# Window masks of four attention units added to the scores in quarter tiles of the TensorE, with new instruction orders

## The chip, the cores and the metric

One core of a Trainium2 chip runs the whole kernel. A core has a matrix engine (TensorE, PE in the profile), a vector engine (VectorE, DVE), an activation engine (ScalarE, ACT), a general engine (GpSimd, POOL) and a queue engine that starts most transfers (SyncE, SP). Each works through its own line of instructions in order; semaphores tie the lines together. PEld in the profile is the loading of matmul weights, which overlaps PE. PSUM is the memory that matmuls write (8 banks per partition), SBUF the one that everything else uses. The metric is the device time of one execution in microseconds, the median of the runs.

## What is computed

Windowed attention with four "sink" keys feeds a channel-mix layer (RWKV's), for 4 batches, 8 heads, 768 tokens, head size 64, model width 512 and hidden width 1024:

```python
scores = q @ k.T / sqrt(64)
keep = is_sink | ((rel >= 0) & (rel < 128))       # rel = query position - key position
a = softmax(where(keep, scores, -1e9))
x = concat_heads(a @ v)                           # (4, 768, 512)
x_prev = x shifted by one token (zero first)
xk = mu_k * x + (1 - mu_k) * x_prev
xr = mu_r * x + (1 - mu_r) * x_prev
k = max(xk @ w_k, 0)
out = sigmoid(xr @ w_r) * ((k * k) @ w_v)
```

## The kernel before

**Tiling.** The work is cut into 12 units: unit u is batch u // 3 and the 256 tokens of third T = u % 3. A unit has four head pairs c. For each unit the kernel loads q, k and v (`ks`, `qs`, `vs`), casts them to bf16 (`kb`, `qb`, `vb`), transposes q and k (`kt`, `qt`; on PE with a copy out of PSUM, or by a transposing transfer for the keys of units 5 to 11 and the queries of 7 to 11), makes the scores, takes the exponential on ACT (L917, `e`), masks it on DVE, multiplies by the values on PE (L950; a column of ones gives the row sums), and divides on DVE (`rec` L964, `x` L967). The mix step transposes `x` to `xt` (PE and a copy, or a transfer for units 6 and 8 to 11) and forms `td` (the difference of neighbouring tokens), `xk` and `xr` on DVE. The channel mix ("ffn") of a unit is 8 hidden products (operations `kp`, four matmuls of 256 columns each, L1117), a relu (`rl`) and a square (`kk`), two gates (`rp`, four matmuls of 512 columns, L1148, `th`), and value products (`vp`, four matmuls of 512 columns each, L1166; two operations per 128 tokens), then `ob` and a store.

**Scores.** Scores of a head pair lie transposed, keys on partitions, queries along the free dimension, in one `sc` tile of [128, 2, 512] floats: two banks, one per head a. There are two such tiles, so one PE operation makes the scores of two head pairs. The 512 columns of a head are four blocks of 128: old keys for the first 128 queries (block 0), the unit's first 128 keys for its first and second 128 queries (blocks 128 and 256), its second 128 keys for its second 128 queries (block 384). For T = 0 block 0 does not exist. The matmuls (L845) run in tiles of 64 x 64: head a takes the row half, 64 keys take the column half, which gives four tiles; quarter blocks that the window never reaches are not computed (the memset L567 gives one of them a zero). Unit 0 (`WHOLE`) alone uses 64 x 128.

**Masks.** For T > 0 operation `masked` (L931) multiplies the exponentials of one head pair, [128, 4, 256] bf16, by a 0/1 mask: 32 operations of 1,024 elements per partition; for T = 0 it uses `mask0`: 16 operations of 768. The kernel also holds a way to add a bias by a full 128 x 128 matmul (`biased`), for units in `BIAS`, which is empty.

**Order.** Every step is an operation with a number (the order of the calls of `P.op`). `ORDER` writes out by hand, for each engine, the order of its operations by number. `CHOICE` names the engine of operations that can run on more than one (casts, copies, relus, stores, and whether a sink product runs in 64 x 64 tiles, "PE/tiles", or in the full array, "PE/full"). `schedule` walks those lines with modelled costs; from its modelled clocks come the physical buffer of each tile and the filler matmuls that keep PE occupied while it would wait (L1226, L1229, L1232; only before 28.5 us by `fill_until`). `FETCH` and the line with `0.58 * cost` belong to that model; they issue nothing themselves. Semaphores follow from the order and the buffers.

**Operations that the prediction names** (number before / after the change): 89 is the cast on DVE of the last quarter of w_v (L654); 236 is the second half of a value product of unit 0 (L1166), which reads it. 286 / 279 is the `xk` of unit 2, head pair 1 (L1040); 374 / 367 is the first hidden product of unit 2 (L1117), which reads it. 215 / 212 is the first hidden product in PE's line (unit 0), 81 / 82 the cast of the second quarter of w_k that it reads.

Of the kernel before, what the change touches and what calls it, by code (L numbers as in the profile page):

```python
# [9 lines left out]
BF16 = mybir.dt.bfloat16  # L10
# [8 lines left out]
    80: "ACT", 81: "POOL", 82: "ACT", 83: "POOL", 84: "POOL", 85: "ACT", 86: "ACT",  # L19
    88: "ACT", 90: "DVE", 96: "POOL", 98: "DVE", 99: "DVE", 101: "DVE", 102: "ACT",  # L20
    103: "ACT", 129: "POOL", 132: "DVE", 135: "POOL", 141: "ACT", 144: "DVE", 151:
    "DVE", 160: "PE/full", 172: "PE/full", 183: "POOL", 186: "DVE", 189: "POOL",
    192: "POOL", 195: "ACT", 196: "DVE", 198: "DVE", 242: "PE/full", 265: "DVE",
    268: "DVE", 271: "POOL", 273: "DVE", 274: "POOL", 277: "DVE", 278: "ACT", 352:
    "POOL", 355: "POOL", 361: "DVE", 380: "DVE", 428: "POOL", 432: "POOL", 438:
    "ACT", 496: "PE/full", 511: "POOL", 516: "ACT", 517: "ACT", 587: "POOL", 591:
    "ACT", 592: "ACT", 628: "POOL", 661: "POOL", 663: "POOL", 665: "ACT", 666:
    "ACT", 675: "DVE", 736: "POOL", 741: "ACT", 785: "POOL", 810: "POOL", 815:
    "DVE", 855: "POOL", 888: "DVE", 889: "ACT", 929: "POOL", 945: "PE/full", 998:
    "DVE", 1002: "DVE", 1006: "DVE", 1010: "DVE", 1019: "POOL",  # L30
# [7 lines left out]
BIAS = ()  # L38
# [7 lines left out]
LOW = -30000.0  # L46

FETCH = (17500.0, 28500.0, 36900.0, 47800.0, 57300.0, 66500.0, 78000.0, 85500.0,
         96000.0, 104000.0, 113000.0, 126000.0, 135000.0, 147000.0, 161000.0)
# [5 lines left out]
TOGETHER = 2  # L55
# [3 lines left out]
WHOLE = (0,)  # L59
# [35 lines left out]
    ),  # L95
    "DVE": (
# [1193 lines left out]
```

## Time and profile before

| | us |
|---|---|
| median of 3 runs | 166.36 |
| lowest and highest run | 165.06, 167.31 |
| span of the profiled execution (first to last instruction) | 163.8 |
| PE busy in it | 154.4 |
| DVE busy | 148.4 |
| ACT busy | 121.4 |
| POOL busy | 32.7 |

The page gives the profiled execution by its span; what lies around it is the 2.6 us between the span and the median of the runs. In a timeline row the columns are start, length, engine, line, operation, output<-inputs, shapes and count, then the idle time before it and what ended that; neighbouring instructions of one kind are merged. An instruction's record includes the draining of its pipeline, so rows of one engine overlap, and the distance from a start to the next start is what it takes of the engine's line.

### The profile page before, as it was taken

The page shows a single profiled execution, that of the slowest core. Times are in us where ns is not written, and L with a number is a line of the kernel's source. Part 1 is how long each engine was busy: PE and PEld are TensorE (multiplying, and loading weights), DVE is VectorE, ACT ScalarE, POOL GpSimd, SP SyncE. Part 2 cuts the span into 40 slices and gives each one's busy share as a digit, 9 for nine tenths or more (in the row PEclk, how much of TensorE's full clock was granted, in tenths as well). Part 3 has the DMA queues.
Part 4 walks back from the last instruction along what each step waited for, and adds up shares of the span by engine and source line. Part 5 has one row for each costly group of instructions (what it writes and reads, how often), then busy time and mean ns, then how long its engine had stood idle before and what let it go on. Part 6 is the DMA issues. An engine that isn't in the chain of part 4 may idle for free.

```text
span 163.8 us, 4680 instructions
## 1 busy us (share of the span) xinstructions
PE 154.4 (94%) x1845; PEld 100.8 (62%) x1845; DVE 148.4 (91%) x383; ACT 121.4 (74%) x198; POOL 32.7 (20%) x61
## 2 busy tenths in 40 slices
PE   7989779899999999999999999999999999999991
PEld 2446458675468558777656666855385756578450
DVE  2589999999999999999999999998898989999931
ACT  3779899999999998999996689882499694152020
POOL 6643543222731022111103001032000100101001
PEclk9999999999999999999999999999999999999998
DMA  4999999999999999999997998979999963251032
GB/s 138 250 334 275 400 346 205 362 397 338 200 289 238 265 233 225 196 179 189 276 233 174 254 196 218 242 188 119 239 162 201 268 79 98 57 203 64 0 144 112
DMA packets 78821, 35.16 MB, mean 215 GB/s; under 512 B 68744, under 2 KB 71056, under 8 KB 78800
## 3 DMA queue, kind: packets, MB, share of 16 engines
q1 hardware_dynamic: 78384, 33.56, 85.8%
q0 software_dynamic: 400, 1.31, 2.3%
q8 instruction: 14, 0.23, 0.6%
q14 instruction: 7, 0.06, 0.1%
q10 hardware_dynamic: 16, 0.00, 0.0%
HBM read 24.12 MB, written 6.29 MB: 186 GB/s over the span
## 4 chain that ended last, share of the span: by engine, by line
PE 69%; DVE 11%; DMA 10%; SPq 5%; issue 2%; ACT 1%; POOL 0%; DVEq 0%; POOLq 0%
PE bank L1117 22%; PE bank L1166 19%; PE bank L1148 9%; PE bank L950 6%; DMA ks<-in_k_dram 5%; PE sc L845 4%; DMA kt<-kb 4%; DVE e L931 3%; SPq L462 3%; PE bank L1232 3%; DVE xk L1040 2%; DVE x L967 2%; PE bank L903 1%; SPq L479 1%; PE bank L991 1%
## 5 line engine op out<-in xcount | busy, mean ns | idle before, releaser
L1117 PE MATMUL bank<-xk,wk_sb 128*128 128x256 bf16 x384 | 47.3, 273 | 0.7 <-ACT rl L1127 0.5
L917 ACT ACTIVATE e<-sc 128x1024 bf16<-128x1024 f32 (+1 forms) x48 | 44.4, 966 | 3.4 <-PE sc L845 3.3
L1166 PE MATMUL bank<-wv_h,kk 128*128 128x512 bf16 x184 | 44.9, 379 | 0.0
L1117 PEld LDWEIGHTS <-wk_sb 128*128 128x128 bf16 x384 | 36.2, 98 | 7.0 <-issue 0.9
L931 DVE TENSOR_TENSOR e<-e,mask 128x1024 bf16<-128x1024 bf16 (+1 forms) x48 | 31.7, 676 | 0.0
L1127 ACT ACTIVATE rl<-bank 128x512 bf16<-128x512 f32 x43 | 25.1, 606 | 8.1 <-PE bank L1117 7.9
L1154 ACT ACTIVATE th<-bank 128x512 f32<-128x512 f32 x24 | 14.3, 608 | 18.2 <-PE bank L1148 11.4
L1166 PEld LDWEIGHTS <-kk 128*128 128x128 bf16 x184 | 17.0, 98 | 16.4
L1148 PE MATMUL bank<-wr_sb,xr 128*128 128x512 bf16 x96 | 23.8, 379 | 0.0
L1040 DVE SCALAR_TENSOR_TENSOR xk<-td,mu_all,xt 128x256 bf16<-128x256 bf16 x48 | 23.2, 511 | 0.0
L1040 DVE SCALAR_TENSOR_TENSOR xr<-td,mu_all,xt 128x256 bf16<-128x256 bf16 x48 | 22.4, 477 | 0.0
L967 DVE TENSOR_TENSOR x<-bank,rec 128x256 bf16<-128x256 f32 x48 | 19.5, 418 | 0.5
L1139 DVE TENSOR_TENSOR kk<-rl 128x512 bf16<-128x512 bf16 x48 | 19.3, 416 | 0.3 <-ACT rl L1127 0.2
L1175 DVE SCALAR_TENSOR_TENSOR ob<-th,bank 128x512 f32<-128x512 f32 x23 | 15.6, 682 | 2.4 <-PE bank L1166 1.1
L950 PE MATMUL bank<-vb,e 128*128 128x65 bf16 x352 | 16.5, 194 | 0.3
L950 PEld LDWEIGHTS <-e 128*128 128x128 bf16 x352 | 13.8, 97 | 3.5 <-DVE e L931 0.7
L1148 PEld LDWEIGHTS <-xr 128*128 128x128 bf16 x96 | 9.0, 98 | 9.6
L845 PE MATMUL sc<-qt,kt 64*64 64x128 bf16 (+3 forms) x496 | 12.6, 226 | 0.4 <-DMA kt<-kb 0.3
L1182 POOL DMA_DIRECT2D out_dram<-ob x5 | 2.8, 570 | 47.0 <-DVE ob L1175 47.0
L845 PEld LDWEIGHTS <-kt 64*64 64x64 bf16 (+1 forms) x496 | 9.0, 106 | 4.1 <-issue 1.4
L1027 DVE TENSOR_TENSOR td<-xt 128x512 bf16<-128x512 bf16 x24 | 10.1, 433 | 0.1
L770 ACT CAST vb<-vs 128x512 bf16<-128x512 f32 x14 | 8.8, 636 | 0.2 <-DMA vs<-in_v_dram 0.2
(93 smaller groups left out, 157.7 us busy)
## 6 DMA issues: line engine op xcount, KB each, us to landing
vs<-in_v_dram SPq DMA_DIRECT2D x24, 256.0 KB, 5.5
out_dram<-ob SPq DMA_DIRECT2D x18, 256.0 KB, 3.4
ks<-in_k_dram SPq DMA_DIRECT2D x16, 256.0 KB, 4.6
qs<-in_q_dram SPq DMA_DIRECT2D x12, 256.0 KB, 4.7
qs<-in_q_dram SPq DMA_DIRECT2D x6, 512.0 KB, 7.5
ks<-in_k_dram SPq DMA_DIRECT2D x4, 512.0 KB, 9.6
w<-in_moe_w_k_dram SPq DMA_DIRECT2D x2, 1024.0 KB, 8.8
w<-in_moe_w_v_dram SPq DMA_DIRECT2D x2, 1024.0 KB, 11.3
```

Of the source, the lines that this page charges most:

```text
L845: nc.tensor.matmul(out=sc[keys, a, o0 + f0 - q0:o0 + f1 - q0], lhsT=lhs[rows, keys], rhs=qs[rows, f0:f1], start=u not in BIAS, stop=True, ...
L917: nc.scalar.activation(out=buf[ek][:, :, lo:], in_=buf[sck][:, :, lo:], func=AF.Exp, scale=scale)
L931: nc.vector.tensor_tensor(out=at, in0=at, in1=m, op=ALU.mult)
L950: nc.tensor.matmul(out=o[:, g, a, :], lhsT=e[:, a, e0:e0 + 128], rhs=rhs, start=(T == 0 and i == 0), stop=(i == len(blocks) - 1), skip_gro ...
L967: P.op("DVE", dve(256), lambda ok=ok, rk=rk, c=c: nc.vector.tensor_tensor(out=buf["x", u][:, :, 128 * c:128 * c + 128].rearrange("p g (a d ...
L1040: nc.vector.scalar_tensor_tensor(out=buf[key][:, c, :], in0=buf[tk][:, i, :], scalar=mu[w][:, c:c + 1], in1=xt[:, c, t0 - 1:t0 + 255], op0 ...
L1117: nc.tensor.matmul(out=ps[:, i, :], lhsT=wk_sb[:, c, 128 * f:128 * f + 128], rhs=xk[:, c, :], start=(c == 0), stop=(c == NC - 1), skip_gro ...
L1127: nc.scalar.activation(out=buf[rk], in_=buf[psk].rearrange("p (i t) -> p i t", i=2), func=AF.Relu)
L1139: P.op("DVE", dve(512, 0.52), lambda f2=f2, rk=rk: nc.vector.tensor_tensor(out=buf["kk", u][:, 2 * f2:2 * f2 + 2, :], in0=buf[rk], in1=buf ...
L1148: nc.tensor.matmul(out=buf[psk], lhsT=buf["xr", u][:, c, 128 * g:128 * g + 128], rhs=wr_sb[:, c, :], start=(c == 0), stop=(c == NC - 1))
L1166: nc.tensor.matmul(out=buf[psk], rhs=wv_h[:, f, :], lhsT=buf["kk", u][:, f, 128 * g:128 * g + 128], start=(f == 0), stop=(f == NF - 1))
L1175: P.op("DVE", dve(512), lambda psk=psk, tk=tk, bk=bk: nc.vector.scalar_tensor_tensor(out=buf[bk], in0=buf[tk], scalar=1.0, in1=buf[psk], o ...
```

## The change

The masks of units 1, 2, 4 and 5 are no longer multiplied into the exponentials. Instead PE adds a bias of 0 or -30000 to the scores before the exponential, by matmuls of a 64 x 64 identity with the bias, in the same four 64 x 64 tiles as the scores: per head pair four matmuls of 256 columns each (head a in the row half, 64 keys in the column half; the moving operand is a quarter of the bias, read twice by a broadcast). 16 DVE operations go. The other eight units keep their masks, and the masks of `mask0` stay.

Quarter blocks that are never computed now hold -30000, set once by memsets (three pieces per `sc` tile instead of one). Where a unit with T = 0 has written into such a block of a tile (unit 0 into three of them, unit 3 into one), the next biased unit that uses the tile adds -30000 there by a matmul of 64 columns for each head (`spoilt`, `fresh`). Scores of a head now start accumulation only with the first block's matmul. The bias tile is made on POOL by two selects; it has its own storage. Filler matmuls no longer use `sc` tiles.

`CHOICE` and all five lines of `ORDER` are new. Numbers shift: one more for operations after the new bias operation (78), one less for each dropped mask. In the new `CHOICE`, by count of operations on each engine (before, after): casts of k on DVE 2, 7, on POOL 13, 8; casts of q on ACT 15, 14, on DVE 4, 3, on POOL 5, 7; casts of v on ACT 14, 6, on DVE 4, 5, on POOL 6, 13; copies of transposed q on ACT 13, 10, on DVE 1, 4; of transposed k on ACT 8, 9, on DVE 2, 1; copies of `xt` on ACT 9, 6, on DVE 5, 8; relus on ACT 43, 44, on DVE 5, 4; casts of w_k on DVE 0, 1, on POOL 2, 1; stores of `ob` by POOL 5, 1, by SP 18, 22 (and the last two by SP as before); sink products in the full array 5, 6. SP's line now loads the keys and queries of unit 1 among those of unit 0 (the second half of unit 0's keys is fifth instead of fourth) and the queries of unit 3 ahead of w_k.

```diff
-BIAS = ()
+BIAS = (1, 2, 4, 5)
-FETCH = (17500.0, 28500.0, 36900.0, 47800.0, 57300.0, 66500.0, 78000.0, 85500.0,
...
+FETCH = (17200.0, 24600.0, 35000.0, 47000.0, 53500.0, 62300.0, 71300.0, 80800.0, 90700.0,
...
-                port[o["engine"]] = t + (0.58 * cost if o["engine"] == "POOL" else cost)
+                port[o["engine"]] = t + (max(0.0, cost - 165.0) if o["engine"] == "POOL" else cost)
...
+    bias = tile1([128, 2, 128], BF16, "bias")
+    spoilt = {}
...
+    unseen = ((0, 64), (1, 128), (1, 384))
...
         for t in P.pools["sc"]:
-            nc.vector.memset(t[0:64, :, 64:128], 0.0)
+            for keys, c0 in unseen:
+                nc.vector.memset(t[64 * keys:64 * keys + 64, :, c0:c0 + 64], LOW)
...
+    def make_bias():
+        window_mask(bias.rearrange("p k q -> p (k q)"), warm[:, 0:128], LOW)
...
+    if BIAS:
+        const_op("POOL", 600.0, make_bias, ["bias"], rank=-51)
...
+            fresh = spoilt.setdefault(id(sc), set())
+            if u in WHOLE:
+                fresh.update(((1, 128), (0, 320), (1, 384)))
+            elif T == 0:
+                fresh.add((0, 320))
...
+            for n, (lhs, o0, q0, q1) in enumerate(jobs):
                 for a in range(2):
                     rows = slice(64 * a, 64 * a + 64)
-                    for keys, f0, f1 in parts:
+                    for half in range(2):
+                        keys = slice(64 * half, 64 * half + 64)
+                        f0, f1 = q0, q1
+                        if half == 0 and o0 < 384 and T > 0:
+                            f1 = max(q1 - 64, q0 + 64)
+                        if half == 1 and o0:
+                            f0 = q0 + 64
                         nc.tensor.matmul(out=sc[keys, a, o0 + f0 - q0:o0 + f1 - q0],
                                          lhsT=lhs[rows, keys], rhs=qs[rows, f0:f1],
-                                         start=u not in BIAS, stop=True,
-                                         skip_group_check=u in BIAS)
...
+                                         start=n == 0, stop=u not in BIAS,
+                                         skip_group_check=True)
+            if u not in BIAS:
+                return
+            for a in range(2):
+                rows = slice(64 * a, 64 * a + 64)
+                for half in range(2):
+                    keys = slice(64 * half, 64 * half + 64)
+                    out = sc[keys, a, :].rearrange("p (g k q) -> p g k q", g=2, k=2)
+                    nc.tensor.matmul(out=out[:, :, :, keys], lhsT=ident[rows, rows],
+                                     rhs=bias[rows, :, rows].unsqueeze(1).to_broadcast(
+                                         [64, 2, 2, 64]),
+                                     start=False, stop=True, skip_group_check=True)
+                for half, c0 in sorted(fresh):
+                    keys = slice(64 * half, 64 * half + 64)
+                    low = bias[rows, a, 64 - 64 * a:128 - 64 * a]
+                    nc.tensor.matmul(out=sc[keys, a, c0:c0 + 64], lhsT=ident[rows, rows],
+                                     rhs=low, start=False, stop=True, skip_group_check=True)
+            fresh.clear()
```

More of the change, by code (lines that the diff above doesn't have):

```diff
@@ L18 @@
 CHOICE = {
[L19 to L30, printed above, removed]
+    81: "POOL", 82: "ACT", 83: "DVE", 84: "ACT", 85: "POOL", 86: "ACT", 87: "ACT",
@@ new lines @@
+    88: "DVE", 89: "DVE", 90: "ACT", 91: "DVE", 93: "ACT", 94: "ACT", 96: "DVE", 97:
+    "DVE", 99: "DVE", 100: "POOL", 102: "ACT", 103: "DVE", 104: "POOL", 130: "POOL",
+    132: "ACT", 133: "DVE", 135: "ACT", 136: "DVE", 138: "ACT", 139: "DVE", 141:
+    "ACT", 142: "DVE", 143: "POOL", 145: "DVE", 152: "DVE", 161: "PE/full", 171:
+    "PE/full", 180: "POOL", 182: "ACT", 183: "POOL", 185: "ACT", 186: "ACT", 188:
+    "ACT", 189: "ACT", 191: "DVE", 192: "POOL", 193: "DVE", 195: "ACT", 202: "DVE",
@@ new lines @@
+    210: "ACT", 214: "ACT", 218: "DVE", 222: "ACT", 231: "POOL", 235: "SP", 239:
+    "PE/full", 249: "PE/tiles", 258: "DVE", 260: "ACT", 261: "ACT", 263: "ACT", 264:
+    "POOL", 266: "ACT", 267: "POOL", 269: "ACT", 270: "ACT", 271: "POOL", 276:
+    "DVE", 283: "DVE", 291: "DVE", 295: "ACT", 299: "ACT", 303: "DVE", 312: "SP",
+    316: "SP", 339: "ACT", 341: "ACT", 342: "POOL", 344: "DVE", 345: "POOL", 347:
+    "ACT", 348: "ACT", 350: "DVE", 351: "POOL", 352: "ACT", 354: "DVE", 361: "ACT",
+    369: "ACT", 373: "ACT", 377: "ACT", 381: "ACT", 390: "SP", 394: "SP", 398:
@@ new lines @@
+    "PE/tiles", 408: "PE/tiles", 417: "POOL", 418: "POOL", 420: "ACT", 421: "ACT",
+    423: "POOL", 425: "ACT", 426: "POOL", 427: "ACT", 429: "ACT", 436: "DVE", 444:
+    "DVE", 448: "ACT", 452: "ACT", 456: "ACT", 465: "SP", 469: "SP", 473:
+    "PE/tiles", 483: "PE/tiles", 492: "ACT", 493: "ACT", 495: "ACT", 496: "DVE",
+    498: "ACT", 500: "ACT", 501: "POOL", 502: "DVE", 507: "ACT", 514: "DVE", 522:
+    "ACT", 526: "ACT", 530: "ACT", 534: "ACT", 543: "SP", 547: "SP", 570: "ACT",
+    571: "ACT", 572: "ACT", 574: "ACT", 576: "POOL", 577: "DVE", 592: "ACT", 596:
@@ new lines @@
+    "ACT", 600: "ACT", 604: "ACT", 613: "SP", 617: "SP", 621: "PE/tiles", 633:
+    "PE/tiles", 644: "DVE", 645: "POOL", 646: "POOL", 648: "ACT", 650: "POOL", 651:
+    "POOL", 653: "ACT", 660: "ACT", 668: "ACT", 672: "ACT", 676: "ACT", 680: "ACT",
+    689: "SP", 693: "SP", 697: "PE/full", 709: "PE/tiles", 720: "POOL", 721: "ACT",
+    722: "ACT", 724: "ACT", 726: "ACT", 727: "POOL", 745: "ACT", 749: "ACT", 753:
+    "ACT", 757: "ACT", 766: "SP", 770: "SP", 793: "ACT", 794: "DVE", 795: "DVE",
@@ L31 @@
+    797: "ACT", 799: "ACT", 800: "ACT", 815: "ACT", 819: "ACT", 823: "ACT", 827:
+    "ACT", 836: "SP", 840: "SP", 844: "PE/tiles", 856: "PE/tiles", 867: "ACT", 868:
+    "ACT", 869: "POOL", 871: "ACT", 873: "POOL", 874: "POOL", 889: "ACT", 893:
+    "ACT", 897: "ACT", 901: "ACT", 910: "SP", 914: "SP", 918: "PE/full", 930:
+    "PE/full", 955: "ACT", 959: "ACT", 963: "ACT", 967: "ACT", 976: "SP", 980: "SP",
+    983: "ACT", 987: "ACT", 991: "ACT", 995: "ACT", 1004: "SP",
 }
@@ L320, in schedule @@
                 while now + 230.0 < t:
-                    some = [(b[0], name, b[1], b) for name in ("bank", "sc") for b in free[name]
-                            if b[0] <= now] + [b for b in own if b[1] in ("bank", "sc") and b[0] <= now]
+                    some = [(b[0], name, b[1], b) for name in ("bank",) for b in free[name]
+                            if b[0] <= now] + [b for b in own if b[1] == "bank" and b[0] <= now]
                     if not some:
@@ L526 @@
     rows8 = early[0:2 * NC, 384:512]
-    bias = [early.bitcast(BF16)[:, 0:384],
-            early.bitcast(BF16)[:, 384:640].unsqueeze(1).to_broadcast([128, 2, 256])]
     for i, src in enumerate((moe_mu_k, moe_mu_r)):
```

47 lines of the change are left out of this document (14 added, 33 removed), and 139 rows, old and new, of the table ORDER.

## The prediction

> **What bounds the kernel now.** I read the page first (busy times and the slices), then the table by stretches, then TensorE's and VectorE's timelines, then the waits.
>
> ```profile
> span 163.8 us, 4680 instructions
> PE 154.4 (94%) x1845; PEld 100.8 (62%) x1845; DVE 148.4 (91%) x383; ACT 121.4 (74%) x198; POOL 32.7 (20%) x61
> PEclk9999999999999999999999999999999999999998
> 10.00:15.00 5.00, 4.25 (x56) 2.43 (x56) 4.81 (x13) 4.08 (x7) 2.21 (x3) 1.00 1.18 329
> 20.00:25.00 5.00, 3.92 (x69) 2.87 (x69) 4.97 (x13) 5.00 (x8) 2.28 (x2) 1.00 1.13 340
> 45.00:160.00 115.00, 114.59 (x1375) 75.95 (x1374) 108.13 (x279) 82.63 (x138) 12.11 (x21) 1.00 0.87 186
> ```
>
> The columns of the stretches are PE, PEld, DVE, ACT and POOL busy, the TensorE clock, the DMA engines' share and GB/s. From 45 to 160 PE is busy 114.59 of 115 us at full clock: it is the bound there. Between 10 and 25 PE has gaps, while DVE has 4.8 to 5.0 of 5 and the DMA share is above 1. So the span is "when PE gets going" plus "the PE work then left", and the early part belongs to DVE and the loads together.
>
> ```profile
> 41.11 2.75 PE L1166 MATMUL bank<-wv_h,kk 128*128 128x512 bf16 x12
> 43.70 0.39 PE L733 MATMUL bank<-ident,qb 128*128 128x128 bf16 x4
> 43.92 1.03 PE L1166 MATMUL bank<-wv_h,kk 128*128 128x512 bf16 x4
> 86.88 0.51 PE L845 MATMUL sc<-qt,kt 64*64 64x192 bf16 x24
> 87.33 0.42 PE L950 MATMUL bank<-vb,e 128*128 128x65 bf16 x8
> 87.58 1.02 PE L1166 MATMUL bank<-wv_h,kk 128*128 128x512 bf16 x4
> 88.44 0.60 PE L1117 MATMUL bank<-xk,wk_sb 128*128 128x256 bf16 x4
> 94.86 2.35 PE L1117 MATMUL bank<-xk,wk_sb 128*128 128x256 bf16 x20
> 97.04 1.03 PE L1166 MATMUL bank<-wv_h,kk 128*128 128x512 bf16 x4
> 158.82 1.46 PE L1087 MATMUL bank<-wv_h,kk 128*128 128x384 bf16 x8
> 42.20 0.68 DVE L654 TENSOR_SCALAR wv_h<-w 128x1024 bf16<-128x1024 f32 x1
> 42.80 0.42 DVE L1027 TENSOR_TENSOR td<-xt 128x512 bf16<-128x512 bf16 x1
> ```
>
> Durations overlap, so I cost an instruction by the distance from its start to the next one's. A pair of score groups takes 0.45 (86.88 to 87.33), a values operation 0.25, four 512-wide products 0.86, four 256-wide ones 0.44 (20 in 2.18 from 94.86 to 97.04), four transposes 0.22 (43.70 to 43.92). The twelve products from 41.11 are three operations; the third, operation 236, starts at 41.11 + 2 x 0.865 = 42.84, and its last input is the weight cast, operation 89, that VectorE runs from 42.20 to 42.88. There DVE and PE meet. From there PE runs without a hole worth naming to 158.82 + 1.46 = 160.28, so 117.4 us of PE work lie behind the meeting.
>
> **The sum, step by step.**
>
> *The adds on PE.* Each pair of groups of units 1, 2, 4 and 5 (8 pairs) gets 16 matmuls of 256 columns in four tiles of 64x64. No such matmul is in the trace. The nearest row is the score pair itself: 24 matmuls, 3,072 columns. One column alone costs 2.18/(20 x 256) = 0.426 ns, so single file they would take 1.31 us; they take 0.45, so the tiles do run side by side. Per tile a pair streams 768 columns (0.33) beside 0.12 of fixed cost. The adds are 512 columns per tile: 0.21 a pair. The first pairs of units 1 and 4 also repair spoilt blocks (at most 256 and 128 columns per tile over the pair: 0.10 and 0.05). Sum 8 x 0.21 + 0.15 = 1.85, half of it (0.9) in units 4 and 5, behind the meeting. Bounds: nothing, if the adds fit into the fixed cost; 0.87 a pair, if tiles of one half of the rows wait for each other (rival C). I take 0.21, the row's own rate. The added weight loads (0.107 each by the row below) lie beside the matmuls, as the 24 of a pair do now; laid end to end those 24 alone would take 2.6. One more sink product in the full mode: +0.1.
>
> ```profile
> L845 PEld LDWEIGHTS <-kt 64*64 64x64 bf16 x480 | 8.4, 107 | 3.0 <-issue 1.4 <-DMA kt<-kb 0.5 <-DVE kt L751 0.3
> ```
>
> By the Trainium skill (TensorE: Matmul & The Clock Gate, Part 3, what overlaps and what doesn't) a weight load overlaps running matmuls only if it is for another row group. By that rule two neighbouring adds of one head would go one after the other, which is rival C; the pair's 0.45 speaks against it.
>
> *The masks taken from DVE, and what comes instead.*
>
> ```profile
> 51.94 0.69 DVE L1131 TENSOR_SCALAR rl<-bank 128x512 bf16<-128x512 f32 x1
> 52.55 0.17 DVE L964 RECIPROCAL rec<-bank 128x4 f32<-128x4 f32 x1
> 52.64 0.39 DVE L1000 COPY xt<-bank 128x512 bf16<-128x512 bf16 x1
> 52.95 0.41 DVE L967 TENSOR_TENSOR x<-bank,rec 128x256 bf16<-128x256 f32 x1
> 53.28 0.42 DVE L1027 TENSOR_TENSOR td<-xt 128x512 bf16<-128x512 bf16 x1
> 53.61 1.29 DVE L931 TENSOR_TENSOR e<-e,mask 128x1024 bf16<-128x1024 bf16 x2
> 54.82 0.48 DVE L1040 SCALAR_TENSOR_TENSOR xk<-td,mu_all,xt 128x256 bf16<-128x256 bf16 x1
> 55.21 1.09 DVE L1139 TENSOR_TENSOR kk<-rl 128x512 bf16<-128x512 bf16 x3
> 56.24 0.69 DVE L931 TENSOR_TENSOR e<-e,mask 128x1024 bf16<-128x1024 bf16 x1
> 30.81 0.42 DVE L770 CAST vb<-vs 128x512 bf16<-128x512 f32 x1
> 31.14 0.41 DVE L1139 TENSOR_TENSOR kk<-rl 128x512 bf16<-128x512 bf16 x1
> ```
>
> A mask costs 0.605 (53.61 to 54.82, two), so 16 give DVE 9.7 us back in all. What counts is how much falls ahead of the new meeting. In the new lines I looked for the PE operation whose DVE input lies deepest in DVE's line against its own place in PE's. It is 367 (first hidden product of unit 2), which waits for 279 (`xk` of unit 2). Ahead of it DVE's line, against the old one up to operation 89, has: 8 masks of 1,024 fewer (-4.84) and one of 768 (-0.47); two casts more (+0.66 at 0.33); two `xt` copies (+0.62), one `td` (+0.33), three `xk` (+1.17 at 0.39), two `kk` (+0.69), three `rl` (+1.83 at 0.61) and a w_k cast at the 0.60 of row 42.20. Sum +0.6: the freed time is filled with later work, not left empty. DVE reaches its mark 0.6 later than 42.8 while PE's mark lies further on.
>
> Ahead of 367 PE's new line holds the same operations as the old one ahead of 236, plus three halves of value products (3 x 0.865 = 2.6) and the adds of units 1 and 2. Work left behind the meeting: 117.4 - 2.6 + 0.9 + 0.1 = 115.8. (Work ahead of 367, by the same prices: 29.5.)
>
> *The start.*
>
> ```profile
> DVE kb L698 <- DMA ks<-in_k_dram: 2.0, 1, 2.0
> DVE kt L756 <- PE bank L738: 1.9, 1, 1.9
> 21.51 1.51 POOL L656 CAST wk_sb<-w 128x1024 bf16<-128x1024 f32 x1 [1.87 <-DMA w<-in_moe_w_k_dram]
> 22.45 1.11 ACT L650 ACTIVATE wk_sb<-w 128x1024 bf16<-128x1024 f32 x1
> 23.41 1.99 ACT L917 ACTIVATE e<-sc 128x1024 bf16<-128x1024 f32 x2
> ```
>
> DVE has two idle waits at the start, 2.0 for the first keys and 1.9 for their second half. The new line puts the memsets (four pieces more) into the first wait and casts of unit 1 into the second, but the keys' second half is now loaded fifth instead of fourth. I take 0.4 earlier, between 0.8 earlier and 0.5 later. So DVE's mark: 42.8 + 0.6 - 0.4 = 43.0.
>
> The loads give a second mark. The first half of w_k lands at 21.51; now a 512 KB load of unit 3 goes ahead of it, at 340 GB/s 1.5 us: 23.0. With ACT's cast (0.96, 22.45 to 23.41) the first hidden product can start at 24.0. From there to 367 PE has 16 half hidden products (7.0), nine of the 512-wide operations (7.8) and 4.0 of scores, values and transposes: 42.8. Two bounds of one height, released by whichever is last: I take 43.3.
>
> PE ends at 43.3 + 115.8 = 159.1 instead of 160.28: -1.2. The tail (two last products, store) stays. Span 162.6; the median of the runs, 166.36, is 2.6 above this span, and I keep that: **165.2 us**.
>
> *At nothing:* the bias tile on POOL (two selects; POOL is busy 20% and unit 1's scores come after 10 us; without that cover, 0.6); the planner's constants (they only choose buffers and filler matmuls, which end by 28.5); ACT's 13 operations less, since ACT is not where PE waits.
>
> *Stores.* Four more go through SP's line, which holds loads and transposes behind them:
>
> ```profile
> 107.99 0.59 SPq L1182 DMA_DIRECT2D out_dram<-ob  x1
> 110.59 1.24 SPq L715 DMA_TRANSPOSE qt<-qb  x1
> 111.94 2.32 SPq L715 DMA_TRANSPOSE kt<-kb  x1
> 118.76 0.53 PE L845 MATMUL sc<-qt,kt 64*64 64x192 bf16 x24 [0.31 <-DMA kt<-kb]
> ```
>
> A store costs SP 0.6 of issue; its real price is the wait for its result with the loads behind it. Between nothing (the transfers have slack) and several us (rival D). I take nothing. Ahead of operation 89 DVE's old line has 34.0 us of work by the rows above, so by 42.8 it has lost some 9. In the new line unit 10's last key cast, on DVE, has 92 us of work ahead of it, so it ends near 101, and its transposes can be issued well before the 111.94 of now, while PE wants them only 3.6 us of work earlier.
>
> **Rivals.**
> - A, *within 2%*, as above: 0.68.
> - B, *clearly faster*: DVE loses less than the old run did, and w_k lands as early as now. Then 367 could start at 41.3 by the loads, PE ends at 157.1, time 163.2; with adds that cost nothing, 162.2. To pass 2% (163.0, about what a measurement of this kernel can tell from no change) both must come. Against it: the DMA share above 1 at 10 to 25. 0.17.
> - C, *slower by the tiles*: the adds serialise in each half of the rows, 1,024 columns (0.44) and four loads of 0.107 each for a pair, 0.87. Behind the meeting 4 x 0.66 = 2.6, and up to as much ahead of it: 167.8 to 170.4. It passes 2% only if units 1 and 2 pay in full. 0.05, since the pair's rate contradicts it.
> - D, *slower by SP's line*: PE waits at a score pair for a transposed key tile, as at 118.76 now (0.31), because a store ahead waits for its `ob`. The tightest place is unit 6, whose last key cast is now DVE's: 52 us of DVE work and the 9 lost put its end near 61, the landing (6.8 after issue at 111.94 by the wait of 118.76) near 68; PE wants it after 54 us of its own work, and it has lost 43.3 - 29.5 = 13.8 by the meeting: 68. Each us over that is a us of the total. Over 2% needs 4.5 us: 169.7. For it: SP serves all in order; against: the run shown has one such hole, of 0.31. 0.10.
>
> **The numbers.** The likeliest is 165.2. A's own range: the marks between 42.4 and 44.5 and the adds between half and double, 164.0 to 167.5. For eight in ten I go to the near part of B and into C and D: 162.7 to 168.8. Faster by over 2%: 0.17 (B). Slower: 0.15 (C where units 1 and 2 pay too, and D). Same: 0.68.
>
> **What would show it.** Right: score pairs of units 1, 2, 4 and 5 take 0.65 to 0.7 from start to next start and the others 0.45; 16 masks of 1,024 are left instead of 32; PE is whole from about 43; DVE's total falls by about 6 us with idle time appearing late, not early. Wrong: pairs near 1.1 (C); waits of PE for `kt` or `qt` landings (D); PE whole from before 41 (B); or holes on PE after 50, which would mean that the new lines are not kept fed and the meeting point isn't the last one.

## The result and the profile after

The changed kernel takes 171.19 us (median of 4 runs, 170.09 to 172.30), the kernel before beside it 166.62. The ratio is 1.029, 95% interval 1.021 to 1.036: slower, by more than the 2% that count. The forecast was 165.2, 162.7 to 168.8, and "same". The profiled execution has a span of 168.7 against 163.8, so 4.9 us are to be found. Ratios with an interval leave out executions that took over 1.5% longer than the fastest of the same kernel, and medians keep them, so a ratio is not always that of the two medians.

From the page of the changed kernel: span, busy times, and the slices (40 equal parts of the span; a digit is the busy share in tenths).

```profile
span 168.7 us, 4796 instructions
PE 154.4 (92%) x1900; PEld 102.2 (61%) x1919; DVE 145.8 (86%) x381; ACT 116.2 (69%) x185; POOL 30.9 (18%) x62
PE   7869979999889998999897999999989999999991
DVE  6468999999999997989979999998999699995641
DMA  4999999999996998999999999999999804313043
```

The table by stretches of the same kernel (columns as in the prediction):

```profile
10.00:15.00 5.00, 3.85 (x64) 2.40 (x68) 4.11 (x10) 4.44 (x8) 1.78 (x4) 1.00 1.03 283
45.00:160.00 115.00, 110.03 (x1359) 73.74 (x1376) 104.53 (x269) 80.48 (x130) 14.03 (x24) 1.00 0.88 177
```

Between 45 and 160 PE now has 5.0 us of holes where it had 0.4. The DMA row is the one that the prediction read only for the start: the transfers are at 9 tenths or more in nearly every slice up to the 31st, in the kernel before as well.

Places of PE's timeline in the changed kernel where it stood, and its last row (start, length, engine, line, operation, shapes; in brackets the idle time and what ended it):

```profile
45.42 0.92 PE L1152 MATMUL bank<-xk,wk_sb 128*128 128x256 bf16 x7 [0.68 <-DVE xk L1075]
46.90 0.38 PE L751 MATMUL bank<-ident,kb 128*128 128x128 bf16 x4 [0.56 <-DVE ob L1210]
...
66.43 0.30 PE L938 MATMUL bank<-vsink,es 64*64 64x130 bf16 x6 [0.69 <-DVE rl L1166]
...
82.57 0.53 PE L876 MATMUL sc<-qt,kt 64*64 64x192 bf16 x24 [0.53 <-DMA kt<-kb]
...
91.46 0.53 PE L876 MATMUL sc<-qt,kt 64*64 64x192 bf16 x24 [0.67 <-DMA kt<-kb]
...
163.29 1.69 PE L1122 MATMUL bank<-wv_h,kk 128*128 128x128 bf16 x12
```

The first row is the forecast meeting point (unit 2's hidden products behind `xk`): 45.4 instead of 43.3. PE ends at 164.98 instead of 159.1. From 45.4 to the end PE is busy for 115.0, so the work left there was sized nearly rightly (115.8). The rest is 2.1 for the late mark and 4.6 for the holes behind it: 159.1 + 2.1 + 4.6 - 0.8 = 165.0.

To see where PE falls behind, I take for each PE operation its start less all PE work ahead of it in PE's line (prices as in the prediction, 143.4 us in all before, 145.3 after). This *lag* grows where PE stands (or where an operation takes longer than its price); a lower one is better. Profiled executions, lag in us, at seven times:

| kernel | 30 | 45 | 60 | 75 | 95 | 122 | 150 us |
|---|---|---|---|---|---|---|---|
| before | 16.3 | 17.2 | 17.2 | 17.3 | 17.0 | 17.1 | 16.8 |
| after | 14.5 | 16.5 | 16.3 | 17.4 | 19.0 | 19.8 | 19.5 |
| whole change, orders of before (`old_lines_b`) | 14.9 | 15.3 | 15.5 | 15.5 | 15.3 | 15.5 | 16.1 |
| after, no adds | 15.6 | 17.1 | 16.9 | 17.3 | 18.2 | 18.7 | 18.4 |
| after, no masks on DVE | 14.0 | 14.2 | 13.9 | 15.0 | 16.4 | 17.2 | 16.9 |
| after, thin stores | 14.8 | 15.9 | 15.7 | 16.0 | 15.7 | 15.6 | 15.3 |
| after, thin stores and no masks | 13.8 | 14.2 | 14.0 | 14.6 | 14.3 | 13.9 | 13.7 |
| after, both repairs (`both_fed`) | 14.0 | 14.9 | 15.7 | 16.5 | 18.5 | 20.2 | 20.0 |
| after, `fed` | 20.6 | 21.3 | 23.5 | 23.4 | 23.4 | 23.2 | 23.8 |

After the change PE does get going earlier (14.5 against 16.3 at 30 us), as forecast. Then it loses 5.0, at many places: 2.0 by 45 us, 3.5 between 60 and 122. At the end it is 2.7 behind the kernel before; with 1.9 of added work that is 4.6 of the 4.9.

### The profile page after: what moved, and what is told of

It reads as the page before. It is cut to its first block, busy times and chain, and to the rows that moved or that the text cites. A ratio compares the mean times of both kernels' runs of the same rounds, so it can differ in the third digit from the quotient of the medians.

```text
span 168.7 us, 4796 instructions
## 1 busy us (share of the span) xinstructions
PE 154.4 (92%) x1900; PEld 102.2 (61%) x1919; DVE 145.8 (86%) x381; ACT 116.2 (69%) x185; POOL 30.9 (18%) x62
## 2 busy tenths in 40 slices
DMA packets 79078, 35.18 MB, mean 209 GB/s; under 512 B 68744, under 2 KB 71056, under 8 KB 79056
## 4 chain that ended last, share of the span: by engine, by line
PE 50%; DVE 26%; DMA 13%; SPq 4%; issue 3%; ACT 2%; POOL 0%; DVEq 0%; POOLq 0%
PE bank L1152 17%; PE bank L1201 15%; PE bank L1183 6%; DMA ks<-in_k_dram 6%; DMA qs<-in_q_dram 4%; PE bank L985 4%; DVE xr L1075 3%; DVE x L1002 3%; DVE xk L1075 3%; DMA kt<-kb 3%; DVE kk L1174 3%; PE sc L876 2%; DVE e L966 2%; DVE td L1062 2%; SPq L482 2%
## 5 line engine op out<-in xcount | busy, mean ns | idle before, releaser
L1152 PE MATMUL bank<-xk,wk_sb 128*128 128x256 bf16 x384 | 48.6, 273 | 0.7 <-DVE xk L1075 0.7
L1201 PE MATMUL bank<-wv_h,kk 128*128 128x512 bf16 x173 | 43.6, 379 | 0.6
L1162 ACT ACTIVATE rl<-bank 128x512 bf16<-128x512 f32 x44 | 26.1, 603 | 24.0 <-PE bank L1152 23.4
L1075 DVE SCALAR_TENSOR_TENSOR xr<-td,mu_all,xt 128x256 bf16<-128x256 bf16 x48 | 23.7, 506 | 0.0
L1183 PE MATMUL bank<-wr_sb,xr 128*128 128x512 bf16 x88 | 22.9, 379 | 0.7 <-DVE xr L1075 0.4
L966 DVE TENSOR_TENSOR e<-e,mask 128x768 bf16<-128x768 bf16 (+1 forms) x32 | 20.3, 650 | 1.1 <-ACT e L952 1.1
L788 POOL CAST vb<-vs 128x512 bf16<-128x512 f32 x13 | 10.0, 768 | 56.0 <-DMA vs<-in_v_dram 55.9
L1210 DVE SCALAR_TENSOR_TENSOR ob<-th,bank 128x512 f32<-128x512 f32 x23 | 15.6, 681 | 3.1 <-PE bank L1201 2.8
L876 PEld LDWEIGHTS <-kt 64*64 64x64 bf16 x480 | 9.1, 106 | 5.9 <-issue 3.6
L1062 DVE TENSOR_TENSOR td<-xt 128x512 bf16<-128x512 bf16 x24 | 10.8, 455 | 0.5 <-DMA xt<-x 0.3
L999 DVE RECIPROCAL rec<-bank 128x4 f32<-128x4 f32 x48 | 7.7, 173 | 1.4 <-PE bank L985 0.8
```

The costliest lines, as they stand in the source:

```text
L876: nc.tensor.matmul(out=sc[keys, a, o0 + f0 - q0:o0 + f1 - q0], lhsT=lhs[rows, keys], rhs=qs[rows, f0:f1], start=n == 0, stop=u not in BIAS ...
L966: nc.vector.tensor_tensor(out=at, in0=at, in1=m, op=ALU.mult)
L1075: nc.vector.scalar_tensor_tensor(out=buf[key][:, c, :], in0=buf[tk][:, i, :], scalar=mu[w][:, c:c + 1], in1=xt[:, c, t0 - 1:t0 + 255], op0 ...
L1152: nc.tensor.matmul(out=ps[:, i, :], lhsT=wk_sb[:, c, 128 * f:128 * f + 128], rhs=xk[:, c, :], start=(c == 0), stop=(c == NC - 1), skip_gro ...
L1162: nc.scalar.activation(out=buf[rk], in_=buf[psk].rearrange("p (i t) -> p i t", i=2), func=AF.Relu)
L1183: nc.tensor.matmul(out=buf[psk], lhsT=buf["xr", u][:, c, 128 * g:128 * g + 128], rhs=wr_sb[:, c, :], start=(c == 0), stop=(c == NC - 1))
```

## The experiments

Ratios are to the kernel before on the same chip, with 95% intervals where there is one.

**SyncE's holds.** In SP's timeline of the changed kernel the queue stood empty from 44.68 to 46.88 (a store that waits for `ob`) and from 48.47 to 52.01 (a transposition that waits for a cast); the kernel before has no such gap there. Waits of SP over 0.4 us come to 7.1 us in all between 40 and 88 us in the changed kernel, and to 5.1, most of them later, in the kernel before.

```profile
42.19 2.49 SPq L482 DMA_DIRECT2D vs<-in_v_dram  x1
46.88 0.36 SPq L1217 DMA_DIRECT2D out_dram<-ob  x1
47.28 0.43 SPq L482 DMA_DIRECT2D vs<-in_v_dram  x1
47.82 0.65 SPq L492 DMA_DIRECT2D ks<-in_k_dram  x1
52.01 1.33 SPq L733 DMA_TRANSPOSE kt<-kb  x1
```

`sp_moved` puts the two behind four loads (first edit), `no_adds` leaves the adds out, so that units 1, 2, 4 and 5 are unmasked (second), `old_lines` has the whole change with `ORDER` and `CHOICE` of the kernel before, renumbered, and the bias tile made behind the mask.

```diff
...
-        25, 312, 26, 32, 422, 34, 30, 316,
+        25, 26, 32, 34, 30, 312, 422, 316,
...
-            if u not in BIAS:
-                return
+            fresh.clear()
+            return
...
```

> Only SP's line is edited: the store of unit 1's first half (operation 312) and the key transposition of unit 5 (422), which hold SP from 44.7 to 46.9 and from 48.5 to 52.0 us in the changed kernel's trace, go behind the loads of unit 6's first keys, its queries and unit 5's values. Theory 1 (SP's line starves the later stages): those loads start some 4 us earlier, the wait of DVE for unit 6's keys at 65.4 us (0.93) and PE's waits for transposed keys and queries at 82.6, 91.5 and 123.5 us (2.2 together) shrink, time 167 to 169. Theory 2 (the adds cost more than costed) and theory 3 (the late start, which is past by then): no more than 0.8 us off 171.2.

> The changed kernel without the bias matmuls: units 1, 2, 4 and 5 get no mask at all (that part of the computation is left out), every line and order as changed. Theory 1: 8 pairs are shorter by about 0.2 us each (1.8 us of PE work), but PE waits for loads and for DVE afterwards, so the time falls by 0.5 to 1.8 us: 169.4 to 170.7. Theory 2 (the adds are the loss): it falls to 168.5 or below. Theory 3: as theory 1.

> The masks by matmuls alone: the changed kernel with the lines and engine choices of the kernel before, numbers shifted, the 16 masks dropped, the bias tile made behind the mask on POOL. PE has 1.9 us more work. Theory 1 (the new lines, above all SP's, lose the time, not the masks): VectorE's marks ahead of the meeting fall by up to 4.8 us, but ScalarE's and the loads' marks there stand within 0.5 us of it, so the start gains little: 166.5 to 168.5. Theory 2 (the adds are the loss): 169.5 or more. Theory 3 (the new order of the first loads costs the start): as theory 1, with PE whole from the time it is in the kernel before.

`sp_moved` took 170.91, 1.028 (1.022 to 1.033): nothing gained. SP now waited 3.8 and 3.1 at the same two kinds of place, 53.4 and 57.8, and its waits between 40 and 88 us came to 9.6. So the run moved the holds and did not take them away: unit 8's keys landed at 90.96 instead of 91.42, and the run can't say what a line without holds is worth. `no_adds` 1.010 (1.004 to 1.017). The old orders gave 168.06 in four executions that differed much, and in a second run, `old_lines_b`, 167.08 in 12, 1.001 (0.997 to 1.005; the median of all 12 is 0.5% above). That is the largest finding: **in the old orders the change costs nothing to within 0.5%; the new orders cost 2.8%.** The expectation of a second run:

> The same kernel as old_lines, once more, with more executions: the whole change in the code, with the orders and choices of the kernel before. Theory 1 (the adds' 2 us of TensorE are mostly paid back by an earlier start): 166.2 to 167.6, and the new orders own most of the loss. Theory 2 (the adds cost what they take): 168 to 169.

**What relief and adds are worth in the old orders.** `old_no_adds` drops the 16 masks and adds nothing; `old_12` has adds in units 1 and 2 alone.

```diff
-BIAS = (1, 2, 4, 5)
+BIAS = (1, 2)
```

> The orders and choices of the kernel before, without the masks of units 1, 2, 4 and 5 on VectorE and without the adds; those units are unmasked. What the relief of VectorE alone is worth in the old lines. Theory 1 (VectorE sets the start and TensorE is whole behind it, so relief ahead of the meeting reaches the end): TensorE's line moves forward by 1.5 and stays there, 164.3 to 165.3. Theory 2 (the landings of units 10 and 11, which stood at the same time in both runs, take the gain back): 165.8 to 166.8.

> The orders of the kernel before, with adds in units 1 and 2 alone; units 4 and 5 keep their masks. Theory 1 (all of the early start is owed to the masks of units 1 and 2, and each unit's adds cost 0.45 of TensorE): about 1 below the run with four units in the old lines, 166.3 to 167.3, and TensorE as early there as with four units. Theory 2 (what counts is VectorE's whole load, later units too): as with four units or above, 167.6 or more.

165.31, 0.985 (0.977 to 0.993, from two of four executions), and 166.59, 1.000 (0.996 to 1.004). Relief alone buys some 1.5% and the adds take as much again. Adds in two units instead of four should be 0.9 us (0.5%) cheaper; 0.1% was measured, and the intervals allow both. Here PE was held at landings of units 9 and 10 (the profiled execution's lag is 16.0 at 95 us and 17.8 at 122; it took 168.0, so it is one of the longer ones). `old_12_sp` loads and transposes these ahead of stores and values:

```diff
...
-        473, 48, 731, 733, 54, 551, 57, 55, 59, 625, 58, 56, 740, 555, 739, 63, 806, 804,
+        48, 731, 733, 473, 54, 57, 55, 58, 56, 551, 59, 625, 740, 739, 806, 804, 555, 63,
...
```

> The orders of the kernel before with adds in units 1 and 2 alone, and the keys and queries of units 9 and 10 loaded and transposed ahead of stores and values in SyncE's line; in the run without that TensorE lost 1.0 at 102.4 and 0.9 at 120, both to landings of these. Theory 1 (the start is won, and only these landings take it back): 165.0 to 165.9, under the kernel before. Theory 2 (the loads' pace sets these marks, and what goes ahead only delays what comes behind): 166.3 or more.

1.007 (1.005 to 1.010): worse. Unit 9's queries landed no earlier (102.44 instead of 102.40). DVE, which waited 2.6 for PE behind that landing, then made PE stand twice more:

```profile
104.12 1.47 PE L1132 MATMUL bank<-xk,wk_sb 128*128 128x256 bf16 x12 [0.76 <-DVE ob L1190]
...
107.02 0.30 PE L918 MATMUL bank<-vsink,es 64*64 64x130 bf16 x6 [0.69 <-DVE x L982]
```

**The start.** `start_back` puts the keys' second half back to fourth place in SP's line, and DVE's cast of unit 1 behind it.

```diff
...
-        0, 1, 6, 3, 2, 7, 4, 5,
+        0, 1, 3, 2, 6, 7, 4, 5,
...
-        70, 71, 91, 96, 136, 97, 115,
+        70, 71, 91, 96, 97, 136, 115,
...
```

> The changed kernel with two places of its start put back: SyncE loads the second half of unit 0's keys fourth and unit 1's first keys behind it, and VectorE casts unit 1's second key half behind unit 0's. Theory 1 (the front of the lines loses the 3 us: the keys that VectorE waits for landed at 9.45 instead of 7.41, so its whole line stands about 1 us late when it reaches the mark): 169.6 to 170.4, and the first hidden product of unit 2 that TensorE starts behind xk moves forward by 0.7 to 1. Theory 2 (later holds take back what is won at the front, as in the run with the store moved): 170.6 to 171.6.

171.22, 1.029 (1.022 to 1.035). The cast of these keys moved from 9.47 to 7.43, but by 11.3 DVE stood where it had stood, waiting for the next tile. Here one load put forward only exchanged one wait for another.

**VectorE.** `no_masks` lets the remaining 32 masks do nothing; `no_masks_sp` moves SP's held entries as well.

```diff
-                nc.vector.tensor_tensor(out=at, in0=at, in1=m, op=ALU.mult)
+                pass
```

> The changed kernel with the masks that are left (units 0, 3 and 6 to 11, 17 us of VectorE) doing nothing; their outputs are unmasked. Theory 1 (TensorE's holes after 42 us are ends of VectorE's line, which is too full): they close, 166 to 168. Theory 2 (the holes are landings of loads and transposed keys in SyncE's line, and VectorE only waits with them): 169.5 or more.

> The changed kernel with the remaining masks doing nothing (units 0, 3 and 6 to 11 unmasked) and SyncE's line relieved: the transposition of unit 5's keys behind the second values' load, the first two stores behind work that does not wait for them. In the run without these masks TensorE's line stood at 13.9 from 26 to 62 us and slid to 16.9 by 104, at landings. Theory 1 (VectorE's line costs the new orders some 2.4 ahead of 62 us, SyncE's line as much again behind it, and each alone is covered by the other): TensorE stays below 15.5 to the end, 165.5 to 167.3, 1.5 to 3 under the run without masks alone. Theory 2 (the late slide is no matter of SyncE's holds; the loads' own pace sets it): within 0.7 of that run, 168 or more.

1.011 (1.004 to 1.018) and 1.013 (1.007 to 1.018). Without the masks PE stands nowhere from 26 to 62 us (lag 14.0 to 13.9), so DVE's line made the 2.4 up to there. Then it loses 3.3, about half of it at the landings of units 7 and 8 (0.4 at 79.9, 1.1 at 88.9). Moving SP's entries did not help: the transposition of unit 6's keys now waited 3.9 for a DVE cast.

**A repair by hand.** `fed` moves three casts from DVE and one from ACT into POOL's line, beside the edit of SP's line.

```diff
...
-    142: "DVE", 258: "DVE", 421: "ACT", 496: "DVE",
+    142: "POOL", 258: "POOL", 421: "POOL", 496: "POOL",
...
```

> The changed kernel, complete, with SyncE's line relieved as in the run beside it and four casts moved to GpSimd's line, which is idle there: from VectorE the first values of unit 1, the first keys of unit 3 and the second keys of unit 6 (1.1 us of VectorE), from ScalarE the second keys of unit 5, on which SyncE's line stood for 3.5. Theory 1 (two lines hold TensorE, each by about 2.5; half a repair of one and a repair of the other): 168.5 to 170. Theory 2 (the losses are spread over many places and any repair is taken back at the next): 170.5 or more.

174.84, 1.049 (1.045 to 1.053): worse, through a mistake of mine. POOL's timeline shows it:

```profile
17.01 1.17 POOL L787 CAST vb<-vs 128x512 bf16<-128x512 f32 x2 [4.33 <-DMA vs<-in_v_dram]
28.55 0.66 POOL L706 CAST kb<-ks 128x512 bf16<-128x512 f32 x1 [8.70 <-DMA ks<-in_k_dram]
```

```profile
30.02 0.61 PE L750 MATMUL bank<-ident,qb 128*128 128x128 bf16 x4 [2.41 <-POOL qb L706]
```

I had put the cast of unit 1's first values, which land at 17, ahead of the second values of unit 0, which had landed before 13; all of unit 0 waited. The first keys of unit 3 (258) held POOL's line in the same way up to 28.55, and PE stood for the cast behind them for 2.41; from 30 to 35 its granted clock was then 0.69. But its lag is a measurement: PE is 6 us later than in the changed kernel at 30 us and then stays at 23.2 to 23.8 from 60 us to the end. The landings came later too (unit 8's keys at 94.9 instead of 91.4), but by less than PE did, and PE meets them no more. SP waited 12.8 between 40 and 88 us here, so the run does not tell whether the transfers' own pace or SP's holds set these landings.

**The transfers.** Landings that do not simply follow PE, and a full DMA row: so perhaps the amount of the transfers. Three runs write 8 of the 128 rows of each 256 KB store; all waits and places stay.

```diff
-out=out[b, s0:s0 + 128, :], in_=buf[bk]
+out=out[b, s0:s0 + 8, :], in_=buf[bk][0:8, :]
```

> The changed kernel with 8 of 128 rows in each store of 256 KB; the other rows of the output are not written, every wait and place stays. Theory 1 (the DMA engines are full from 5 to 130 us, and their pace sets the landings of units 7 to 11 on which TensorE stood): these waits go and the time falls by 1.5 to 3, to 168 to 169.7. Theory 2 (the order of the engines' lines sets them, not the traffic): 170.3 to 171.5.

> The kernel before with 8 of 128 rows in each store of 256 KB, as the control. Theory 1 (its landings have slack but for unit 10, which stood at the same time as TensorE's line): 0.3 to 1 less, 165.4 to 166.4. Theory 2 (the engines' lines): no change, 166 to 167. If the transfers bound the old lines as hard as the new ones, it falls by as much as the changed kernel does.

> The changed kernel with thin stores and without the masks that are left (units 0, 3 and 6 to 11 unmasked). TensorE's line stood at 13.9 until 62 us without the masks and then slid to 16.9 at landings. Theory 1 (VectorE and the transfers together are the whole loss): it stays under 15.2, 164.8 to 166.8. Theory 2: as without the masks, 167.5 to 168.8.

The changed kernel falls to 168.44, 1.018 (1.012 to 1.023, which still touches the 1.021 to 1.036 of full stores); the kernel before to 0.996 (0.993 to 0.9995), a third as much. Without masks too it is 165.22, 0.994 (0.989 to 0.998). The table by stretches of the kernel with both, then PE's longest waits in it (us in all, times, longest):

```profile
45.00:160.00 115.00, 113.06 (x1379) 75.21 (x1393) 90.85 (x243) 80.99 (x132) 14.71 (x23) 1.00 0.80 136
```

```profile
PE bank L1267 <- DVE warm L1288: 1.1, 1, 1.1
PE bank L751 <- DVE qb L707: 1.0, 1, 1.0
PE bank L1152 <- ACT wk_sb L668: 0.5, 1, 0.5
```

No landing is left among them, and the lag is 13.7 to 14.6 from 30 us to the end. Thin stores alone keep PE at 15.3 to 16.0 behind 45 us. (The profiled execution took 166.4 us where the median is 168.4, so its row of the table is some 1 to 2 us better than the median.) SP's waits between 40 and 88 us are hardly shorter with thin stores (6.3 instead of 7.1), and yet the transposition of unit 8's keys is issued at 83.31 instead of 87.00. So with less work on DVE and fewer bytes the new orders have next to no holes behind 45 us. That these two are the whole loss of the new orders is not shown: the old orders with both taken away did not run, and they too gain from each alone.

**Repairs in the complete kernel.** `sp_free` casts the second keys of unit 5 on ACT 3 us earlier and moves the three held entries of SP's line far enough back; `dve_fed` moves two `xt` copies and a w_v cast from DVE to ACT, which stood idle for 3.1 us at 43.3; `both_fed` does both.

```diff
...
-        25, 312, 26, 32, 422, 34, 30, 316, 37, 31, 33, 39, 35, 45,
+        25, 26, 32, 34, 30, 312, 37, 31, 422, 33, 39, 35, 316, 45,
...
-        87, 329, 308, 227, 90, 306, 270, 339, 369, 341, 348, 347, 334, 377, 381, 421,
+        87, 283, 329, 276, 308, 227, 90, 89, 306, 270, 339, 369, 341, 348, 421, 347, 334, 377, 381,
...
```

> The changed kernel with SyncE's holds of 2.2, 3.5 and 0.8 between 44.7 and 56.4 us taken out: ScalarE casts the second keys of unit 5 some 3 us earlier, in its idle time, their transposition and unit 1's two stores stand behind loads that wait for nothing. Theory 1 (those 6 us of empty queue are what makes units 7 and 8 land late): TensorE no longer stands at their landings and the time falls by 1 to 2, 169 to 170. Theory 2 (VectorE's line is as late, so the repair is covered): 170.3 to 171.5.

> The changed kernel with two copies and one weight cast (0.34, 0.34 and 0.6 of VectorE) moved to ScalarE's line, which stood idle for 3.1 at 43.3: VectorE reaches the last xk of unit 2 some 1.3 earlier. Theory 1 (both lines hold TensorE): little at the end, 170.2 to 171.2, with TensorE earlier by 1 at 47 us and held later at landings. Theory 2 (VectorE alone holds it): 169.3 to 170.

> Both repairs at once, the kernel complete. Theory 1 (two lines, each covering the other): more than the two alone together, 167.5 to 169.3. Theory 2 (taken back at the next mark): 170 or more.

1.030 (1.023 to 1.037), 1.030 (1.021 to 1.040), and both 169.75, 1.022 (1.016 to 1.028). Neither alone does anything. Both together are 0.7% lower, but the intervals overlap (1.021 to 1.036 without a repair), and 169.75 lies between the two theories, so no gain is shown. In `both_fed` PE is earlier up to 75 us and is then held again by unit 7 (0.7 at 81.8), unit 8 (0.6 at 90.9) and unit 11 (1.2 at 123.9). SP's holds were not taken away here either. The two of the changed kernel are gone, but a new one of 5.8 stands in their place: unit 6's second keys had landed at 58.57, DVE casts them only at 64.86, and their transposition goes at 65.33.

```profile
58.76 0.81 SPq L1216 DMA_DIRECT2D out_dram<-ob  x1
65.33 1.24 SPq L732 DMA_TRANSPOSE kt<-kb  x1
64.86 0.41 DVE L710 CAST kb<-ks 128x512 bf16<-128x512 f32 x1
```

In every trace of the new orders SP waits 4.7 us or more between 40 and 88 us, where `old_lines_b` has 1.3. No run took these waits away, so what they cost stays untested. The last run moves two stores and a load of unit 9 (entries 394, 390 and 49) behind unit 8's keys (647):

```diff
...
+        647, 394, 390, 49,
...
```

> The changed kernel with both repairs and, in SyncE's line, unit 2's two stores and the first keys of unit 9 behind the transposition of unit 8's keys: about 2.6 less of transfers ahead of units 7 and 8. Theory 1 (the order of the transfers in the new line makes units 7 and 8 late): TensorE stands at neither, 168 to 169.2. Theory 2 (the sum of the transfers counts; what goes behind delays units 9 and 11 as much): 169.4 to 170.5.

176.58, 1.060 (1.050 to 1.070). It does not tell its theories apart. PE's timeline:

```profile
90.37 1.01 PE L1200 MATMUL bank<-wv_h,kk 128*128 128x512 bf16 x2 [4.36 <-DVE ob L1209]
```

There are three `ob` tiles. With two stores held back DVE had none to write to (its wait for a store was 4.6), the PSUM bank stayed taken, and PE stood for 4.4. From 90 to 95 its granted clock was then 0.50, and 0.90 from 95 to 100, so the run lost by the hole and by slower products behind it. So it stays open whether the order of the transfers ahead of unit 8 or only their sum makes its keys late. What the traces show is that the new line has 58 entries of SP ahead of these keys' transposition where the old one has 54, and issues it at 87.00 instead of 76.14, while PE's line asks for them after 72.4 us of work instead of 69.7.

No version was faster than the kernel before: `old_12` and `old_lines_b` are equal to it.

## Why the prediction was wrong, step by step

**What bounds the kernel.** "From there PE runs without a hole", so one meeting point and PE's work behind it: the picture was true of the kernel before and was taken for a property of any line. This is the step that failed. In the kernel before, DVE (94% busy behind 45 us) and the transfers (0.9 to 1.2 in every 10 us up to 135) were near full, and yet the tiles that PE wants were there in time: the transposed keys and queries of units 6 to 9 and 11 landed 1.6 to 6.9 us ahead of PE (unit 8's at 79.98, asked for at 86.88), unit 10's just then. The new orders used that up: unit 8's land at 91.42, and PE takes them at 91.46. The prediction quoted the rows of DVE and the transfers and priced later places at nothing; the holes there are the 4.6 us of the sum above, beside a mark 2.1 late. It had named the sign itself: "holes on PE after 50 ... the meeting point isn't the last one".

**The start, 0.4 earlier.** Half right. PE's line stood 1.8 earlier at 30 us. But DVE's mark came at 45.37 (two `xk` from 43.79 for 1.58) instead of 43.0. The loads' mark was 1.0 late as well: the first half of w_k landed at 23.63 (23.0 forecast), and the first hidden product started at 25.00 (24.0).

```profile
25.00 1.25 PE L1152 MATMUL bank<-xk,wk_sb 128*128 128x256 bf16 x10
43.79 1.58 DVE L1075 SCALAR_TENSOR_TENSOR xk<-td,mu_all,xt 128x256 bf16<-128x256 bf16 x2
43.53 0.82 POOL L707 CAST qb<-qs 128x512 bf16<-128x512 f32 x1 [2.53 <-DMA qs<-in_q_dram]
44.29 0.80 POOL L788 CAST vb<-vs 128x512 bf16<-128x512 f32 x1
```

The two `xk` at the mark took 0.83 each while POOL cast beside them. In this trace the 75 `xk` and `xr` with no POOL operation beside them take 0.477, the 21 with one 0.634 on average. The new `CHOICE` gave POOL 13 casts of v instead of 6, so some 0.7 of the late mark may come from there; no run tests it.

DVE's waits at the start did not shrink; the two of 2.0 and 1.9 became five:

```profile
6.75 0.69 DVE L774 COPY qt<-bank 128x512 bf16<-128x512 bf16 x1 [1.44 <-PE bank L756]
7.80 0.43 DVE L707 CAST kb<-ks 128x512 bf16<-128x512 f32 x1 [0.36 <-DMA ks<-in_k_dram]
9.47 0.57 DVE L716 CAST kb<-ks 128x512 bf16<-128x512 f32 x1 [1.24 <-DMA ks<-in_k_dram]
...
10.91 0.43 DVE L707 CAST qb<-qs 128x512 bf16<-128x512 f32 x1 [0.41 <-DMA qs<-in_q_dram]
...
13.10 0.69 DVE L815 TENSOR_TENSOR vsink<-bank,hmask 128x512 bf16<-128x512 f32 x1 [0.49 <-PE bank L811]
```

That is 3.9 of idle time, as much as before, where the prediction had other work fill it. DVE's total fell by 2.6 (148.4 to 145.8), not by the 6 that it named: the masks' records fell by 11.4, and more copies, casts and slower `xr` (0.506 each against 0.477) took the rest.

**The adds on PE.** Right. In the timeline of the changed kernel:

```profile
61.52 0.36 PE L876 MATMUL sc<-qt,kt 64*64 64x192 bf16 x12
61.71 0.28 PE L887 MATMUL sc<-bias,ident 64*64 64x256 bf16 x4
61.83 0.34 PE L876 MATMUL sc<-qt,kt 64*64 64x192 bf16 x12
61.99 0.28 PE L887 MATMUL sc<-bias,ident 64*64 64x256 bf16 x4
62.10 0.34 PE L938 MATMUL bank<-vsink,es 64*64 64x130 bf16 x8
```

From 61.52 to 62.10 a pair takes 0.58, another 0.66 (55.93 to 56.59), against 0.45 without adds and 0.65 to 0.7 forecast. (A pair has 8 added matmuls, not the 16 that the text says; the 512 columns per tile of its sum are those of 8.) In time they cost 1.6% in the old orders (0.985 to 1.001) and 1.8% in the new (1.010 to 1.029), 2.7 and 3.1 us, above the 1.85 forecast but not by more than the intervals.

**Rival C**, the tiles one after the other, fell: four adds take 0.12 (61.71 to 61.83), where 1,024 columns in single file would be 0.44 by the prediction's 0.426 ns. By the Trainium skill (TensorE: Matmul & The Clock Gate, Part 3, what overlaps and what doesn't) a weight load overlaps running matmuls only for another row group; two of the four have the same one, and they lay beside each other all the same. The trace decides.

**Stores at nothing, and rival D.** SP did stand for a store (2.2) and for a cast (3.5), and PE did wait for landings of keys, at units 7 and 8, not at 6. These waits of PE are 1.2 of its 5.0 us of holes (1.8 with the 0.61 at 123.47, just behind the landing of unit 11's queries at 123.42), so D alone is not the loss. D's price, each microsecond of a landing for one of the total, stays untested: `sp_moved` shifted SP's holds, unit 8's keys landed hardly earlier (90.96), and PE was later itself by 60 us (lag 19.3 instead of 16.3). D was too narrow: DVE's results held PE as well (0.68, 0.56 and 0.69 in the rows above).

**At nothing: POOL's bias tile, ACT's operations, the tail.** Nothing speaks against these. ACT is 69% busy, and span less PE's end is 3.7 against 3.5.

**Transfers.** The prediction quoted 0.87 behind 45 us and put the transfers at nothing there. By the Trainium skill (Perfetto Trace Analysis, Identifying the Most-Contended Engine) the occupancy of the 16 DMA engines misleads, and one is to use HBM utilisation and then find which DMA resource binds. This trace has 35.18 MB in 168.7 us; an estimate from that page's peak for a core (section Engine Utilization, 358 GB/s) is 209 of 358, or 58%. Here the occupancy told more: with 16% of the bytes away (29.53 MB) all of PE's waits for transposed keys went, and with them some 1.1% of the changed kernel's time. What binds the transfers was not looked for.

## What to carry to other kernels

An engine that is busy without a hole is the bound of that order of work, not of the kernel: before reckoning with one meeting point, look how near the next engine and the transfers are in the same stretches, and give a new order a price. Test a change of the arithmetic in the old order first: here it was neutral there, and the loss lay in the orders made for it. When a repair gives nothing, look in its trace whether it took the wait away or only moved it: here SyncE's holds moved each time.

## What the runs showed of the hardware

The issue of the same kind of transfer on SyncE took very different times in the changed kernel. A 256 KB load of v took 0.44 at 128.76 and 2.49 at 42.19, and two took 6.55 from 29.63. Two transposing transfers took 2.50 from 138.00, where the DMA share is 0.14 (135 to 140 us), and one alone 3.21 at 76.06 (queries of unit 7), where it is 1.29 (75 to 80). So SP's line can be held by its issues where it waits for no semaphore.

Four 64 x 64 matmuls of 256 columns, two in each row half, start within 14 ns of each other (61.713 to 61.727), and the next matmul starts 0.12 us after the first.

Behind long holes of PE the granted clock fell: 0.69 from 30 to 35 us behind a hole of 2.41 (`fed`), 0.50 from 90 to 95 behind one of 4.36 (`both_fed_8`). In the changed kernel, whose longest hole between 45 and 160 us is 0.69, it is 1.00 there.

One execution of `sp_free` was granted 0.66 of TensorE's clock from 5 us on and took 231.5 us (PE busy 220.0 of its span of 229.8), the other three of the same kernel 169.9 to 171.4.
